# Retention ahead of a gated feed-forward block: the first six chunks in blocks of 64 tokens, values scaled in place of keys, and the first weights loaded on 128 partitions and earlier

## The chip, the cores and the metric

The kernel runs on one core of one Trainium2 chip. The metric is device microseconds of one execution. Before the change three runs gave a median of 663.18 us (662.83 to 664.07). The profile is of one execution of its own.

The engines are named as in the profile: PE is TensorE's matrix products and PEld its weight loads, DVE is VectorE, ACT is ScalarE, POOL is GpSimd, SP is SyncE, which issues most transfers. Each engine works through its own queue in the order in which the program issued it, and waits for others through semaphores.

## What is computed

```python
# retention: batch 4, 8 heads, 768 tokens, head width 64
gamma = 1.0 - 2.0 ** (-5.0 - np.arange(H))
for t in range(S):
    state = gamma[None, :, None, None] * state + np.einsum('bhd,bhe->bhde', k[:, :, t], v[:, :, t])
    y[:, :, t] = scale * np.einsum('bhd,bhde->bhe', q[:, :, t], state)
# the heads side by side give x: 3072 tokens x 512
h = x @ w_in                      # w_in 512 x 2048
sp = np.maximum(h, 0.0) + np.log1p(np.exp(-np.abs(h)))
out = (h * erf(sp)) @ w_out       # w_out 2048 x 512
```

q, k and v are 32-bit. The two weights are 64-bit floats, and the kernel has to turn them into 32-bit ones itself.

## The kernel before

**Retention.** The 24 chunks of 128 tokens are numbered j = 0 to 23, six to a batch (NC = 6); the first four (JPC = 4) make up the first 512 tokens (TCH) of the feed-forward block. A chunk is computed as scores (keys times queries), a mask, a product of masked scores with values, a product of the running state with queries, and an addition of keys times values to the state. The decay of the heads is put in by scaling keys by one factor and queries by another, per token and head (kq_s), so that the mask has only ones and zeros.

Chunks 0 to 3 are done whole: ret_scale (K_) scales keys and queries on DVE, ret_transpose (T) turns each by four PE transposes and one ACT copy, ret_scores (S_) does eight products of 128x128, ret_mask (M) two DVE operations of 128x512, ret_out (O_) the products with state and values, the state additions and two ACT copies into xT (XC), and ret_add (A) adds to the state on DVE. Their order is written out by hand: the scores of a chunk are issued ahead of the results of the chunk before it. keep_warm issues idle products into one bank.

Chunks 4 and 5 are done in halves of 64 tokens (sub_begin, sub_states, sub_results, sub_sums): 64x64 products, four of which use the array at a time, two states to a chunk, and results of which one part is kept aside in a bank and added by DVE (sub_sums). From chunk 6 on, keys and queries come in blocks of 32x32 by 32 small transfers a chunk (load_blocks, from j = NB = 6), DVE scales them (prepared: the keys for the state, the key blocks, the query blocks) and transposes them, and each chunk is one visit (sub_visit), in which TensorE also does the scores of the chunk after it.

**Feed-forward.** The first 512 tokens are done plainly: hidden (hidden_of, block ft of 128 of the 2048 hidden units) in 16 blocks, four to a group g, then project. hidden_of for blocks 0 and 1 takes the first 384 tokens before the fourth chunk is done and the last 128 after it. From group 4 (G0) on, tokens come in 256 at a time with sums of weights and inputs in place of some of the products (hidden_steps, project_part), and each group of these has one visit.

**Weights.** load_piece brings a piece of W_in (two blocks ft) or W_out into one of four raw buffers; conversion turns a piece into 32-bit floats by five DVE operations (lines 313, 317, 322, 325 and 331 of the listing) and one ACT activation, a Relu on line 314, which reads what the first DVE operation wrote and is read by the fourth. Piece 0 is converted in four parts, two halves of its rows for each block. A raw buffer is loaded again (load_pieces_after) when its conversion has read it. These steps are taken one at a time (pace) between other DVE work, and need("in", ft) takes as many as are missing.

**Order of transfers.** SP issues, in order: keys and queries of chunk 0; then for each further chunk its keys and queries and the values of the chunk before; W_in's piece 0, first block, then the values of chunk 3, then piece 0, second block; pieces 1 to 3; chunk 4. W_in goes to 64 partitions at a time, rows 0 to 255 in the lower half and 256 to 511 in the upper, which goes with the order in which heads are put into xT.

The order in the head, as it stands in the code (one row for what follows one another there):

```python
K_(0, 0); second_scales(); T(0, 0); keep_warm(2); K_(0, 1); T(0, 1); keep_warm(1)
K_(1, 0); T(1, 0); S_(0); K_(1, 1); T(1, 1); keep_warm(2); other_scales(); M(0); S_(1)
K_(2, 0); T(2, 0); O_(0); M(1); K_(2, 1); T(2, 1); A(0); K_(3, 0); O_(1, next_scores)
T(3, 0); K_(3, 1); A(1); T(3, 1); O_(2, lambda: next(weight_steps)); S_(3)
need("in", 0); A(2); M(3); need("in", 1)
ret_out(JPC - 1, lambda: hidden_of(0, slice(TCH - C)), state_last=True)
```

Of the kernel before, what the change touches and what calls it, by code (L numbers as in the profile page):

```python
# [136 lines left out]
def kernel(  # L137
# [42 lines left out]

    def load_blocks(to, src):


        for s, d in itertools.product(range(2), range(2)):
            part = slice((2 * s + d) * 32, (2 * s + d + 1) * 32)
            for u in range(HP):
                nc.sync.dma_start(
                    to[part, u * C : (u + 1) * C].rearrange("p (a d) -> p a d", d=32),
                    src[2 * u + s, :, d * 32 : (d + 1) * 32].rearrange("(a p) d -> p a d", p=32),
                )  # L190

    def load(j):
# [15 lines left out]
        for i, src in enumerate((k, q) if j < NB else ()):  # L208
            nc.sync.dma_start(KQ[j][:, i], src[b, :, now, :].rearrange("h p d -> p h d"))
# [46 lines left out]
    def load_piece(n, *parts):  # L256
# [3 lines left out]
        if which == "in":  # L260
            rows = (slice(2), slice(2, 4)) if n == 0 else (slice(4),)
            for part, g, r in itertools.product(parts or (None,), rows, range(2)):
                f = slice(2 * P) if part is None else slice(part * P, (part + 1) * P)
                nc.sync.dma_start(
                    w[r * D : (r + 1) * D].rearrange("p (g f) -> p g f", g=n_k)[:, g, f],
                    w_in[r * DH : (r + 1) * DH, i * 2 * P : (i + 1) * 2 * P].rearrange(
                        "(g p) f -> p g f", p=D
                    )[:, g, f],
                )
# [134 lines left out]

    for j in range(1, JPC):
        load(j)
        load_values(j - 1)
    load_piece(0, 0)
    load_values(JPC - 1)
    load_piece(0, 1)  # L410
    for n in range(1, 4):
# [4 lines left out]
    causal = const.tile([P, C], F32, name="causal")  # L416
    nc.gpsimd.memset(causal, 1.0)
    nc.gpsimd.affine_select(
        out=causal, in_=causal, compare_op=ALU.is_ge, fill=0.0,
        base=0, pattern=[[1, C]], channel_multiplier=-1,  # L420
    )

    causal_d = const.tile([P, D], F32, name="causal_d")
    for r in range(2):
        own = slice(r * D, (r + 1) * D)
        nc.gpsimd.tensor_copy(causal_d[own], causal[own, own])
    state = const.tile([P, HP, D], F32, name="state")


    state_1 = const.tile([P, HP, D], F32, name="state1")  # L430
    state_2 = loads.tile([P, HP * C], F32, name="kb", bufs=2)[:, : HP * D]
    state_2 = state_2.rearrange("p (u d) -> p u d", d=D)
    mid = [state, state_1, state_2, state, None, state_1]
    adds_of = {JPC: range(2), JPC + 1: range(1), JPC + 2: range(1)}
    assert (JPC + 2) % NC == 0 and NC > 1


    unscale = 1.0 / math.sqrt(D)

    def query_scale(c):  # L440
        nc.vector.reciprocal(kq_s[:, c, 1], kq_s[:, c, 0])
# [20 lines left out]
    kq_b = const.tile([P, NC, 2, HP, 4], F32, name="kq_b")  # L462
    by_b = const.tile([P, 2, HP], F32, name="by_b")

    def load_block_scales():
        for s, d in itertools.product(range(2), range(2)):
            part = slice((2 * s + d) * 32, (2 * s + d + 1) * 32)
            for u in range(HP):
                nc.sync.dma_start(
                    kq_b[part, 0, 0, u],  # L470
                    decay_k[:, 2 * u + s : 2 * u + s + 1].rearrange("(a p) h -> p (a h)", p=32),
                )
        nc.sync.dma_start(by_b[:, 1], decay_s)

    def block_scales():
        nc.vector.reciprocal(by_b[:, 0], by_b[:, 1])
        nc.vector.reciprocal(kq_b[:, 0, 1], kq_b[:, 0, 0])
        nc.vector.tensor_scalar(kq_b[:, 0, 1], kq_b[:, 0, 1], unscale, None, op0=ALU.mult)
        for c in range(1, NC):
            nc.gpsimd.tensor_tensor(  # L480
                kq_b[:, c], kq_b[:, c - 1], by_b[:, :, :, None].to_broadcast([P, 2, HP, 4]),
                op=ALU.mult,
# [3 lines left out]
    QT, KT, SC, AM, XC, SU = {}, {}, {}, {}, {}, {}  # L486
# [4 lines left out]
    idle = ps_o.tile([P, P], F32, name="o0")  # L491

    def keep_warm(n):
        for _ in range(n):
            nc.tensor.matmul(idle, ident, ident, start=True, stop=True)

    keep_warm(7)
# [8 lines left out]
    def ret_scale(j, i=None):  # L506
# [3 lines left out]
        scaled.add(j)  # L510
        part = slice(i, i + 1) if i is not None else slice(2)
        x = KQ[j][:, part]
        by = kq_s[:, j % NC, part, :, None].to_broadcast([P, x.shape[1], H, D])
        nc.vector.tensor_tensor(x, x, by, op=ALU.mult)
        pace(-1.1)

    def ret_transpose(j, part=None):
        assert j in scaled
        for i, (name, store) in enumerate((("k", KT), ("q", QT))):
            if part not in (None, i):  # L520
                continue
            p = ret_psum((ps_h if i else ps_r) if early else None)
# [10 lines left out]
    def prepared(j):  # L533

        if j >= NJ:
            return
        nc.vector.tensor_tensor(
            KQ[j][:, 0], KQ[j][:, 0],
            kq_s[:, j % NC, 0, :, None].to_broadcast([P, H, D]), op=ALU.mult,
# [3 lines left out]
        for i, x in enumerate(blocks):  # L543
            x = x.rearrange("p (u a d) -> p u a d", u=HP, d=32)
            by = kq_b[:, j % NC, i, :, :, None].to_broadcast([P, HP, 4, 32])
            nc.vector.tensor_tensor(x, x, by, op=ALU.mult)
            yield
# [5 lines left out]
    def ret_scores(j, pool=None):  # L553
        pp = SC[j] = [ret_psum(pool) for _ in range(2)]
        for hp in range(HP):
            for s in range(2):
                nc.tensor.matmul(  # L557
                    pp[s][:, hp, :],
                    KT[j][s * D : (s + 1) * D, hp, :],
                    QT[j][s * D : (s + 1) * D, hp, :],  # L560
                    start=True,
                    stop=True,
                )
        pace(1)

    def ret_mask(j):
        AM[j] = ret.tile([P, 2, HP, C], F32, name="am")
        for s in range(2):
            nc.vector.tensor_tensor(
                AM[j][:, s], SC[j][s], causal[:, None, :].to_broadcast([P, HP, C]), op=ALU.mult  # L570
            )
        pace(-1.2)

    def ret_out(j, between=None, state_last=False):
        c = j % NC
        m, i = divmod(j, JPC)
        if i == 0:
            XC[m] = ret.tile([P, HP, TCH], F32, name="xT")

        if early:  # L580
            pp = [ps_o.tile([P, HP, C], F32, name=f"o{(2 * j + r + 1) % 4}") for r in range(2)]
        else:
            pp = [ret_psum() for _ in range(2)]

        def place(h):
            return pp[h % 2][h // 4 * D : (h // 4 + 1) * D, h % 4 // 2, :]

        if state_last:
            between()


        if c:
            for u in PAIRS:
                for r in range(2):
                    h = 2 * u + r
                    own = slice(r * D, (r + 1) * D)
                    nc.tensor.matmul(
                        place(h), state[own, u, :], QT[j][own, u, :],
                        start=(h % 4 < 2), stop=False, skip_group_check=True,
                    )  # L600
        if between is not None and not state_last:
            between()
        for h in (0, 4, 1, 5, 2, 6, 3, 7):
            nc.tensor.matmul(  # L604
                place(h), V[j][:, h, :], AM[j][:, h % 2, h // 2, :],
                start=(not c and h % 4 < 2), stop=True, skip_group_check=True,
            )
# [105 lines left out]
    def sub_visit(j, g):  # L713
# [44 lines left out]
        if c:  # L758
            of_state(0)
# [590 lines left out]
```

## Time and profile before

| what | us |
|---|---|
| median of three runs | 663.18 |
| span of the profiled execution | 660.9 |
| PE busy (share of the span) | 655.7 (99%) |
| DVE busy | 508.4 (77%) |
| ACT busy | 280.2 (42%) |
| POOL busy | 11.7 (2%) |

| stretch, us from the start | what runs in it | PE busy | DVE busy | ACT busy | DMA, GB/s |
|---|---|---|---|---|---|
| 0 to 31.7 | chunks 0 to 3, hidden blocks 0 and 1 | 29.37 | 23.02 | 11.86 | 204 |
| 31.7 to 164 | the rest of the first 512 tokens, chunks 4 to 6 | 132.30 | 122.79 | 73.11 | 158 |
| 164 to 627 | groups with a visit | 462.95 | 343.90 | 187.68 | 51 |
| 627 to 660.9 | the last projections | 31.07 | 18.65 | 7.54 | 31 |

A busy PE is one whose products overlap without a gap by the profile; it says where PE doesn't wait, not that it works at its peak. In the rows of the timeline the columns are the start, the length, the engine, the line, the operation, what it writes and reads, the tile, how many were merged into the row, and in brackets how long the engine was idle before it and who ended that. A 32-bit product stands in the trace as two records, a transpose as one. Starts that lie less than a length apart are pipelined: the distance of two starts is what one more of them costs.

### The profile page before, as it was taken

How to read it: one execution, taken by the hardware profiler on the slowest of the kernel's cores; microseconds unless marked ns; L12 is line 12 of the kernel's file. 1: busy time of each engine (PE TensorE's matmuls, PEld its weight loads, DVE VectorE, ACT ScalarE, POOL GpSimd, SP SyncE). 2: the span in 40 equal slices, each digit the busy share in tenths (PEclk: the TensorE clock that was granted, in tenths of full speed). 3: DMA queues.
4: the chain of work that ended last, by engine and by line, in shares of the span. 5: the costliest groups of instructions: out<-in, count | busy, mean ns of one | idle time of the engine just before them, and what ended most of it. 6: DMA issues, size and time to landing. Idle time of an engine off the chain costs nothing.

```text
span 660.9 us, 15247 instructions
## 1 busy us (share of the span) xinstructions
PE 655.7 (99%) x6200; PEld 557.3 (84%) x6200; DVE 508.4 (77%) x1102; ACT 280.2 (42%) x402; POOL 11.7 (2%) x29
## 2 busy tenths in 40 slices
PE   8999999999999999999999999999999999999998
PEld 7744444576999999999999999999999999999997
DVE  5999999969986786788678678677687688476464
ACT  3468363445534334244254253342432542533440
POOL 1000000110100000000000000000000000000000
PEclk9999999999999999999999999999999999999999
DMA  9999844385753321222222322221231210000000
GB/s 188 223 264 231 211 129 107 63 152 90 144 123 61 85 47 32 67 47 46 70 44 47 73 39 46 42 72 37 44 79 36 46 53 1 2 34 0 1 33 32
DMA packets 159413, 51.88 MB, mean 78 GB/s; under 512 B 143216, under 2 KB 149744, under 8 KB 159344
## 3 DMA queue, kind: packets, MB, share of 16 engines
q1 hardware_dynamic: 157776, 46.72, 32.8%
q0 software_dynamic: 1152, 4.19, 3.4%
q8 instruction: 48, 0.79, 0.5%
q14 instruction: 21, 0.17, 0.1%
q10 hardware_dynamic: 416, 0.01, 0.0%
HBM read 40.39 MB, written 6.29 MB: 71 GB/s over the span
## 4 chain that ended last, share of the span: by engine, by line
PE 98%; DMA 1%; DVE 0%; ACT 0%; issue 0%
PE o L1034 37%; PE hp L951 22%; PE r L951 12%; PE hp L860 8%; PE o L896 8%; PE hp L980 2%; PE r L736 2%; PE hp L628 1%; PE o L772 1%; PE r L524 1%; PE r L557 1%; PE o L604 1%; PE r L751 1%; PE hp L751 1%; DMA kq<-in_k_dram 1%; PE r L772 0%
## 5 line engine op out<-in xcount | busy, mean ns | idle before, releaser
L1034 PE MATMUL o<-w_out_sb,h 128*128 128x256 f32 (+1 forms) x640 | 142.7, 380 | 0.0
L951 PE MATMUL hp<-xs,w_in_sb 128*128 128x128 f32 x988 | 138.1, 275 | 0.0
L1034 PEld LDWEIGHTS o<-w_out_sb,h 128*128 128x128 f32 x640 | 119.5, 190 | 16.6
L963 DVE TENSOR_TENSOR h<-h,hp 128x256 f32<-128x256 f32 x190 | 78.0, 418 | 70.5 <-PE hp L951 65.6
L951 PEld LDWEIGHTS hp<-xs,w_in_sb 128*128 128x128 f32 x988 | 128.4, 192 | 3.0
L1034 PE MATMUL o<-w_out_sb,e 128*128 128x256 f32 x480 | 113.5, 379 | 0.0
L1034 PEld LDWEIGHTS o<-w_out_sb,e 128*128 128x128 f32 x480 | 86.8, 190 | 9.4
L817 ACT ACTIVATE e<-h 128x2048 f32<-128x2048 f32 x22 | 42.1, 1912 | 119.6 <-DVE h L963 119.6
L963 DVE TENSOR_TENSOR h<-h,r 128x256 f32<-128x256 f32 x152 | 56.9, 415 | 22.3 <-PE r L951 21.4
L965 ACT COPY h<-hp 128x256 f32<-128x256 f32 x38 | 14.2, 373 | 130.7 <-PE hp L951 122.7
L951 PE MATMUL r<-xs,w_in_sb 128*128 128x128 f32 x456 | 63.3, 275 | 0.0
L951 PEld LDWEIGHTS r<-xs,w_in_sb 128*128 128x128 f32 x456 | 57.0, 192 | 0.0
L860 PE MATMUL hp<-xT,w_in_sb 128*128 128x512 f32 (+2 forms) x144 | 56.5, 548 | 0.0
L849 DVE TENSOR_TENSOR e<-h,e 128x1024 f32<-128x1024 f32 x42 | 49.2, 1213 | 8.0 <-ACT e L830 8.0
L860 PEld LDWEIGHTS hp<-xT,w_in_sb 128*128 128x128 f32 x144 | 25.8, 190 | 27.0 <-issue 24.6
L951 PE MATMUL hp<-xT,w_in_sb 128*128 128x128 f32 x304 | 46.3, 275 | 0.0
L951 PEld LDWEIGHTS hp<-xT,w_in_sb 128*128 128x128 f32 x304 | 41.5, 192 | 1.4 <-issue 0.5
L830 ACT ACTIVATE e<-e 128x2048 f32<-128x2048 f32 (+1 forms) x23 | 42.1, 1836 | 0.2
L967 ACT ACTIVATE h<-hp 128x256 f32<-128x256 f32 x57 | 21.9, 384 | 29.7 <-PE hp L951 28.3
L951 PE MATMUL r<-xT,w_in_sb 128*128 128x128 f32 x228 | 31.7, 275 | 0.0
L830 ACT ACT_TABLE_LOAD x24 | 30.8, 1283 | 0.4
L951 PEld LDWEIGHTS r<-xT,w_in_sb 128*128 128x128 f32 x228 | 28.5, 192 | 0.0
(164 smaller groups left out, 799.0 us busy)
## 6 DMA issues: line engine op xcount, KB each, us to landing
w_out_sb<-in_moe_w_out_dram SPq DMA_DIRECT2D x14, 512.0 KB, 5.2
kq<-in_k_dram SPq DMA_DIRECT2D x23, 256.0 KB, 4.0
v<-in_v_dram SPq DMA_DIRECT2D x23, 256.0 KB, 3.4
out_dram<-r SPq DMA_DIRECT2D x23, 256.0 KB, 2.9
kq<-in_q_dram SPq DMA_DIRECT2D x288, 16.0 KB, 1.9
kb<-in_k_dram SPq DMA_DIRECT2D x288, 16.0 KB, 1.8
w_in_sb<-in_moe_w_in_dram SPq DMA_DIRECT2D x8, 512.0 KB, 10.1
w_out_sb<-w_out_sb POOLq DMA_DIRECT2D x8, 512.0 KB, 5.3
```

The source lines that it names most:

```text
L736: nc.tensor.matmul(pp[r][col * D : (col + 1) * D, u % 2, t], x[own, u, :], QT[j][own, u, t], start=first(r, col), stop=True, skip_group_ch ...
L751: nc.tensor.matmul(other[a][own, u % 2, D:] if crossed else pp[a][own, u % 2, t], V[j][t, 2 * u + r, :], AM[j][t, r, u, :D], start=crossed ...
L817: nc.scalar.activation(E[g], HS[g], AF.Softplus)
L830: nc.scalar.activation(E[g][:, half], E[g][:, half], AF.Erf)
L849: nc.vector.tensor_tensor(E[g][:, half], HS[g][:, half], E[g][:, half], op=ALU.mult)
L860: nc.tensor.matmul(HP_[ft][:, t], w_in_of(ft, kk), XC[0][:, kk, t], start=(kk == 0), stop=(kk == n_k - 1),)
L896: nc.tensor.matmul(O[0][tt].rearrange("p (d c) -> p d c", d=2), E[g][:, u * TCH + tt * P : u * TCH + (tt + 1) * P], w_out_of(ft), start=(f ...
L951: nc.tensor.matmul(to[:, u, :], w_in_sb[:, s, w, u * P : (u + 1) * P], XS[m](x), start=first and u == 0, stop=True, skip_group_check=True,)
L963: nc.vector.tensor_tensor(h, h, of, op=ALU.add if plus else ALU.subtract)
L965: nc.scalar.copy(h, of)
L967: nc.scalar.activation(h, of, AF.Copy, scale=-1.0)
L1034: nc.tensor.matmul(O[m][i][:, half, at], G[g][a][:, u * P : (u + 1) * P], w_out_sb[:, s, OUT[b], u, at], start=i not in started, stop=(s = ...
```

## The change

All chunks are now done in halves of 64 tokens, with the same functions (score_banks, scores, additions, sub_masks, sub_adds, sub_results, sub_sums). Chunks 0 to 3 are issued one after the other. For them the crossed values go first into the bank of the results, ACT reads one element of it, and then states and straight values are added in the same bank, so that no sum is left to DVE; a function given as "between" is issued after that read. keep_warm takes a new tile in the first bank at each call. The values are scaled in place of the keys (V[j] in ret_scale and prepared), so that the keys can be transposed as they come, and the key blocks need no scaling any more; a small transfer of their factor is gone, and POOL makes it by two copies. Four states are kept in turn in place of three.

W_in goes to 128 partitions, one transfer for each part in place of two; to fit this, the heads are taken in another order (head, slot), and keys and queries of chunks 0 to 5 are loaded by two transfers each (load_heads). W_in's piece 0, both blocks, is issued ahead of chunk 3. Values are issued after the keys and queries of their own chunk. In a visit the additions and scores of the next chunk come first, then all results of this one. The result banks of a visit are those that were the banks of the next scores before, and the other way round. sub_sums of chunk 4 comes two steps earlier, together with the states of chunk 5.

```diff
+    def load_heads(to, src):
+        for s in range(2):
+            nc.sync.dma_start(to[:, s * HP : (s + 1) * HP], src[s::2].rearrange("h p d -> p h d"))
...
-            for part, g, r in itertools.product(parts or (None,), rows, range(2)):
+            for part, g in itertools.product(parts or (None,), rows):
                 f = slice(2 * P) if part is None else slice(part * P, (part + 1) * P)
                 nc.sync.dma_start(
-                    w[r * D : (r + 1) * D].rearrange("p (g f) -> p g f", g=n_k)[:, g, f],
...
+                    w.rearrange("p (g f) -> p g f", g=n_k)[:, g, f],
+                    w_in[:, i * 2 * P : (i + 1) * 2 * P].rearrange("(g p) f -> p g f", p=P)[:, g, f],
                 )
...
+    load_values(0)
     for j in range(1, JPC):
+        if j == JPC - 1:
+            load_piece(0, 0, 1)
         load(j)
-        load_values(j - 1)
-    load_piece(0, 0)
-    load_values(JPC - 1)
-    load_piece(0, 1)
+        load_values(j)
...
+        for i in range(2) if i is None else (i,):
+            scaled.add((j, i))
+            x = KQ[j][:, 1] if i else V[j]
+            by = kq_s[:, j % NC, i, :, None].to_broadcast([P, H, D])
+            nc.vector.tensor_tensor(x, x, by, op=ALU.mult)
+            pace(-0.6)
...
+    def sub_begin(j, pool=None):
+        score_banks(j, pool)
+        scores(j)
+        additions(j)
+        pace(1)
...
+        if between is not None:
+            values(True)
+            nc.scalar.copy(idle_out, pp[0][:, 0, D : D + 1])
+            between()
+        if j % NC:
+            of_state(0)
+        values(False)
+        if between is None:
+            values(True, aside=True)
+        of_state(1)
...
+        score_banks(j + 1)
+        additions(j + 1)
+        scores(j + 1)
+        sub_results(j)
+        sub_states(j + 1)
+        sub_sums(j)
...
-                    waiting.append((sub_states, 5))
-                elif g == 2 and tt == 2:
-                    waiting.append((sub_sums, 4))
+                    waiting.extend(((sub_states, 5), (sub_sums, 4)))
```

The order in the head is now:

```python
T(0, 0); K_(0, 1); keep_warm(2); T(0, 1); K_(0, 0); keep_warm(1)
sub_begin(0); second_scales(); sub_masks(0); T(1, 0); sub_adds(0); K_(1, 1)
sub_results(0, lambda: keep_warm(1)); T(1, 1); K_(1, 0); other_scales()
sub_begin(1); sub_masks(1); sub_adds(1, slice(1)); K_(2, 1)
sub_results(1, lambda: T(2, 0)); sub_adds(1, slice(1, 2)); K_(2, 0); T(2, 1)
sub_begin(2); sub_masks(2); sub_adds(2, slice(1)); next(weight_steps)
sub_results(2, lambda: keep_warm(1)); T(3, 0); need("in", 0)
sub_adds(2, slice(1, 2)); K_(3, 1); hidden_of(0, first); T(3, 1); K_(3, 0)
need("in", 1); hidden_of(1, first, slice(2)); sub_begin(3, ps_r); sub_masks(3)
hidden_of(1, first, slice(2, 3)); sub_adds(3)
sub_results(3, lambda: hidden_of(1, first, slice(3, 4)))
```

K_(j, 0) scales the values of chunk j, K_(j, 1) its queries, T(j, 0) transposes its keys and T(j, 1) its queries; first is the first 384 tokens.

## The prediction

> **What bounds the kernel now.** I read the chain of waits first, then TensorE's waits before and after 60 us, then busy time by stretch, then the first 37 us engine by engine.
>
> ```profile
> span 660.9 us, 15247 instructions
> PE 98%; DMA 1%; DVE 0%; ACT 0%; issue 0%
> ```
>
> The chain is TensorE almost alone. So the time is the start of its unbroken run plus the work in that run. Its waits, first those within 60 us:
>
> ```profile
> PE o L495 <- POOL ident masks.py:199: 1.5, 1, 1.5
> PE o L597 <- DVE state L806: 0.3, 1, 0.3
> PE r L524 <- DVE kq L514: 0.3, 1, 0.3
> PE r L557 <- ACT qT L530: 0.2, 1, 0.2
> ```
>
> The same view from 60 us to the end is empty. A change can thus move the time in two ways: by TensorE work after the head, or by the moment at which the head is done. As the mark of that moment I take the first 512-wide product of weight block 2:
>
> ```profile
> 27.27 7.25 PE L860 MATMUL hp<-xT,w_in_sb 128*128 128x384 f32 x30
> 31.74 1.50 PE L860 MATMUL hp<-xT,w_in_sb 128*128 128x512 f32 x3
> ```
>
> From 31.74 us TensorE does not pause again. The columns of the next view are the stretch, then busy us of PE, PEld, DVE, ACT and POOL, the clock, the DMA share, GB/s:
>
> ```profile
> 25.00:30.00 5.00, 5.00 (x58) 3.52 (x58) 4.83 (x14) 2.38 (x5) 0.00 (x0) 1.00 1.13 231
> 30.00:35.00 5.00, 5.00 (x25) 3.31 (x24) 4.86 (x11) 2.36 (x4) 0.00 (x0) 1.00 1.14 234
> 40.00:45.00 5.00, 5.00 (x13) 2.22 (x12) 4.72 (x9) 4.89 (x5) 0.00 (x0) 1.00 1.00 354
> ```
>
> VectorE is as full as TensorE here: it converts the 64-bit weights, five operations a block. Its queue:
>
> ```profile
> 19.37 0.29 DVE L313 TENSOR_SCALAR w_out_sb<-w_out_sb 128x256 uint32<-128x256 uint32 x1 [0.35 <-DMA w_out_sb<-in_moe_w_in_dram]
> 22.52 0.43 DVE L325 SCALAR_TENSOR_TENSOR w_out_sb<-w_out_sb 128x256 uint32<-128x256 uint32 x1 [0.35 <-ACT w_out_sb L314]
> 30.30 0.69 DVE L331 SCALAR_TENSOR_TENSOR w_in_sb<-w_out_sb,xs 128x512 f32<-128x512 f32 x1
> 33.35 0.69 DVE L331 SCALAR_TENSOR_TENSOR w_in_sb<-w_out_sb,xs 128x512 f32<-128x512 f32 x1
> ```
>
> Conversion starts at 19.37, when its weights land, and then idles 0.35 us in all. Block 2 is ready at 30.99 (30.30 + 0.69), 0.75 us ahead of its use at 31.74. So the head has two limits within a microsecond of each other, and 0.75 us is all that a later VectorE may cost for nothing.
>
> **The change, part by part.** *TensorE work in chunks 0 to 3.* A chunk of 128 took 1.09 (scores, 15.49 to 16.58), 0.92 (values), 0.57 (state additions) and 0.60 (state products): 3.18 us, 2.58 without state products. In blocks of 64, by the rows of chunks 4 and 5, it is 0.51 scores, 0.58 additions, 0.46 values, 0.52 state products: 2.07, and 1.81 for chunk 0. That is 0.77 + 3 x 1.11 = 4.1 us less, and one idle product (0.2 to 0.4) less. It counts only where TensorE waits for nothing else.
>
> *VectorE work in the head.* Eight scalings of 0.6 remain (values instead of keys). Eight masks go from 0.6 apart to 0.33; state additions go from four to eight of about 0.35; the reciprocals of the other chunks go from one of 0.35 to four of 0.20. Sum: -2.2 + 1.4 + 0.45, about nothing. What matters is where it stands in the queue.
>
> *Order.* Before, the scores of a chunk were issued ahead of the results of the one before. Now each chunk runs alone: transposes, ScalarE copy, scores and additions, masks, values, results. I walk the four queues with the durations above and 0.03 to 0.16 us from an end to who waits. Scores start at 8.0, 12.8 and 17.8; a round of chunk 1 is scores and additions 12.8 to 13.9, masks from 14.0, values from 14.8, keys of chunk 2 transposed to 15.7, states and values to 16.45, queries transposed to 17.0, ScalarE's two result copies and then the query copy to 17.8. A round is 5.0 us with 1.8 us of TensorE waiting. Masks of chunk 2 end at 19.8 and the first conversion starts at 20.1. The earlier load of W_in (it would land near 17) buys nothing, since conversion stands behind those masks: 0.7 us later than 19.37.
>
> *What stands between conversion and block 2.* Before, from 19.37 to 30.99, the queue also held one state addition (0.33) and two masks (1.2): 1.5 us, with 0.5 idle (0.35 in the row at 22.52, the rest at 20.42). Now it holds three additions (1.1), two scalings of chunk 3 (1.2) and two masks (0.7): 3.0, so 1.5 more. And it waits four times. Conversion's second operation on ScalarE (L314 before) now stands in ScalarE's queue behind a transpose copy that is behind two result copies: 1.0 us at 22.7. Again behind the query copy of chunk 3, which TensorE can transpose only after the first hidden block: 0.7 at 27.0. The masks of chunk 3 wait for scores that TensorE issues only after half of hidden block 1, itself waiting for weights: 0.9 at 30.2. And behind the result copies of chunk 3: 1.2 at 34.1. Together 3.8, against 0.5. Block 2 is ready at 30.99 + 0.7 + 1.5 + 3.3 = 36.5; the walk itself, step by step, gives 36.7. TensorE, which has by then done both first hidden blocks and their last 128 columns (to 36.4), starts at 36.7 where it started at 31.74: 5.0 us later. Its 4.1 us saved are lost in these waits.
>
> *Loads.* The key and query loads of six chunks become 24 issues on SP for 12 (0.44 each at the start), W_in's 28 become 14 (0.6 each), and one small scale load goes; four of W_in's are moved past chunk 3's three loads. POOL gets two small copies and five products of half the size, first wanted at 122: nothing. The page's loads were in flight 4 to 5 us and came 1.2 us apart, so issue hides behind the queue; chunk 0's second halves land as before (4.34 for keys). If that cover were gone, 0.45 us twice. W_in on 64 partitions ran at 231 to 234 GB/s, W_out at 354 in the window from 40. For 128 partitions I bound it by these two; either lands block 1's weights before 27 us, and they are wanted at 32.6: nothing on the path. Chunk 3's loads slip behind W_in's 1 MB by 3 to 4.5 us, to some 20 to 23, and are wanted at 21.9 (keys) and 24.8: 0 taken, 1 at worst.
>
> *New small waits.* The one-element ScalarE read after the crossed values: 0.2, as the 128x1 copy at 3.05; covered by the idle product or transposes, except in chunk 2 (0.6, in the walk). A fresh bank for idle products makes them wait for TensorE itself: no row, 0 to 0.2 three times, I take 0.1.
>
> *After the head.* A visit has the same 112 or 128 small products in another order; no wait is there to lose and the operands are ready a group earlier: 0, bounded by 0.2 either way for each of 17 if one order packs worse (the visit at 304.88 takes 1.79 for 112). Eighteen key-block scalings (0.6 each) leave VectorE: nothing, it is busy 344 of 463 us there. Values, loaded last, are now scaled first: the wait at 139.30 was for that load's neighbour, so 0 to 0.3. The W_out block needed at 84.6 was ready at 83.7 (its last step, 82.46 + 1.23); VectorE slips 0.6 more than TensorE, so 0.3 remain: 0 taken, 0.4 at worst.
>
> Sum: 31.74 to 36.7, plus 0.1 to 0.3 of small waits: +5.2. The profiled execution would go from 660.9 to 666.1; the median of the runs is 2.3 above that span, and 663.18 + 5.2 = 668.4.
>
> *The clock.* The first 14 idle records take 3.36 us, 0.24 each; the same product from 9.89 on takes 0.11, and in between, four records from 6.02 take 0.85 and four from 6.87 take 0.52. [...] By the rows TensorE stays busy from 1.5 to 7.5 us as before (slow records fill it), and I keep 7 us. [...]
>
> **The rivals.** *TensorE alone sets the head (faster).* If ScalarE let the conversions through and masks came at once, the head would cost its TensorE work: 36.7 less the 9.0 us of waits in my walk is 27.7, so 31.74 - 27.7 = 4.0 us sooner, 659.2. For it: TensorE's queue hardly waits today. Against it: VectorE has 23 us of work of its own between 2.9 and 36.7, most of it in an order in which it can't start early. It decides if block 2 is converted by 28 us.
> *A draw.* If only the four waits vanish, VectorE is 0.7 + 1.5 - 0.5 late, less 0.75 of cover: about +1; with the rounds shortened by 1 as well it is nothing, 663.2.
> *Slower still: late loads.* Eleven loads 1.2 apart from 4.34 are in at 16.4, and 256 KB of W_in at 234 GB/s take 1.1, yet conversion waited until 19.37: W_in's first packets cost 1.9 us more than their bytes. If chunk 2's values or chunk 3's keys are caught in that, each microsecond past 16 or 22 goes straight into conversion: +2, 670.4.
> *The visits cost.* 17 x 0.2 = 3.4 more: 671.8; the packing of like rows speaks against it.
>
> **How the numbers follow.** Forecast (conversion late) 0.66; late loads or clock 0.15; visits 0.04; draw 0.05; faster 0.10. The forecast's own range is 666.5 to 669.8 (the waits behind ScalarE vary by their order, 0.5 each). Reaching to late loads and part of the draw: 665.2 to 671.0. A measurement of this kernel can tell 0.2% (1.3 us) from no change: faster 0.10, same 0.05, slower 0.85.
>
> **What would show it.** First conversion near 20.1 us; VectorE waiting three times for ScalarE's relu of conversion (L325 of the new file) by 36 us; first 512-wide product near 36.7; no TensorE wait after it; group length 25.9 as before; W_in faster than 300 GB/s without use. I am wrong if that product starts before 33, or if visits change the length of a group.

## The result, and the profile after

The changed kernel takes 670.09 us (median of 4 runs, 669.69 to 671.59), the kernel before 663.03 in the same session (4 runs, 662.83 to 664.07): ratio 1.011, 95% interval 1.0095 to 1.0124, that is 7.06 us slower. The forecast was 668.4 with a range of 665.2 to 671.0.

The page of the profiled execution, its first line, its row of granted clock in 40 slices, and its chain of waits:

```profile
span 668.5 us, 15750 instructions
...
PEclk9899999999999999999999999999999999999999
...
PE 96%; DVE 1%; ACT 1%; DMA 1%; issue 0%; SPq 0%; DVEq 0%
```

The chain is still TensorE, but one slice (16.7 to 33.4 us) has lost clock, which no slice had before. TensorE's waits up to 60 us, the longest first (sum, times, longest):

```profile
PE hp L754 <- DVE w_in_sb L342: 3.0, 3, 2.1
PE o L640 <- DVE am L596: 2.0, 3, 0.9
PE r L569 <- ACT qT L544: 1.8, 3, 0.7
...
PE hp L754 <- ACT xT L676: 0.5, 1, 0.5
```

Before, these waits came to 0.8 us but for the 1.5 us for the identity at the start. Now TensorE waits for converted weights, for masks and for ScalarE's copies. The same view from 60 us on is empty, as before. TensorE's rows around the mark that the prediction used:

```profile
28.84 2.68 PE L754 MATMUL hp<-xT,w_in_sb 128*128 128x384 f32 x4 [2.09 <-DVE w_in_sb L342]
31.45 1.14 PE L569 MATMUL r<-qT,kT 64*64 64x64 f32 x32
32.36 0.70 PE L579 MATMUL r<-e 64*64 64x64 f32 x32
...
39.00 6.25 PE L754 MATMUL hp<-xT,w_in_sb 128*128 128x512 f32 x14 [0.34 <-DVE w_in_sb L342]
```

The first 512-wide product of block 2 starts at 39.00 in place of 31.74. Taking the start of the same product in both traces, the offset is 7.26 there, 7.29 from 54 to 136 us, 7.31 up to 170, 7.44 after the first visit, 7.59 to 7.62 from 216 (the kernel before's time) to 583, and 7.43 at the end. So the head makes the difference, and the seventeen visits together less than 0.2.

VectorE's rows in the head, with what ended its idle time in brackets:

```profile
20.31 0.28 DVE L324 TENSOR_SCALAR w_out_sb<-w_out_sb 128x256 uint32<-128x256 uint32 x1
23.81 0.42 DVE L336 SCALAR_TENSOR_TENSOR w_out_sb<-w_out_sb 128x256 uint32<-128x256 uint32 x1 [0.89 <-ACT w_out_sb L325]
27.81 0.43 DVE L336 SCALAR_TENSOR_TENSOR w_out_sb<-w_out_sb 128x256 uint32<-128x256 uint32 x1 [0.71 <-ACT w_out_sb L325]
33.12 0.75 DVE L596 TENSOR_TENSOR am<-r,causal 128x256 f32<-128x256 f32 x2 [2.76 <-PE r L579]
37.44 0.69 DVE L336 SCALAR_TENSOR_TENSOR xs<-w_out_sb,xs 128x512 uint32<-128x512 uint32 x1 [1.38 <-ACT xs L325]
```

These are the first conversion and the four waits of the forecast: 1.0, 0.7, 0.9 and 1.2 were predicted, 0.89, 0.71, 2.76 and 1.38 are there. The one that is off is the masks of chunk 3. ScalarE's rows ahead of the second and the last of these waits show the relu of conversion (L325) directly behind copies that had waited for TensorE:

```profile
26.78 0.58 ACT L544 COPY qT<-r 128x512 f32<-128x512 f32 x1 [3.00 <-PE r L538]
27.26 0.51 ACT L325 ACTIVATE w_out_sb<-w_out_sb,below 128x256 uint32<-128x256 uint32 x1
...
36.14 0.65 ACT L676 COPY xT<-o 128x256 f32<-128x256 f32 x2 [1.47 <-PE o L653]
36.67 0.73 ACT L325 ACTIVATE xs<-xs,below 128x512 uint32<-128x512 uint32 x1
```

Busy time by stretch, with the clock behind POOL's column, shows what happened in front of them:

```profile
28.50:29.00 0.50, 0.16 (x1) 0.19 (x2) 0.50 (x3) 0.07 (x1) 0.00 (x0) 1.00 1.09 348
29.00:30.00 1.00, 1.00 (x2) 0.44 (x2) 0.93 (x4) 0.44 (x1) 0.00 (x0) 0.53 1.11 345
...
32.00:32.50 0.50, 0.50 (x32) 0.50 (x28) 0.00 (x0) 0.00 (x0) 0.00 (x0) 0.52 1.29 226
32.50:33.00 0.50, 0.50 (x37) 0.43 (x29) 0.00 (x0) 0.00 (x0) 0.00 (x0) 1.00 1.30 224
```

The clock was granted at half from 29.07 to 32.48, just after the wait of 2.09 us. Four records of 128x384 take 2.68 there and 1.56 a few us earlier.

### The profile page after: what moved, and what is told of

Same layout as the page of the kernel before. It is cut to its first block, busy times and chain, and to the rows that moved or that the text cites. A ratio compares the mean times of both kernels' runs of the same rounds, so it can differ in the third digit from the quotient of the medians.

```text
span 668.5 us, 15750 instructions
## 1 busy us (share of the span) xinstructions
PE 655.4 (98%) x6454; PEld 554.7 (83%) x6454; DVE 496.8 (74%) x1092; ACT 280.3 (42%) x406; POOL 10.9 (2%) x30
## 4 chain that ended last, share of the span: by engine, by line
PE 96%; DVE 1%; ACT 1%; DMA 1%; issue 0%; SPq 0%; DVEq 0%
PE o L924 37%; PE hp L841 22%; PE r L841 11%; PE o L786 8%; PE hp L754 8%; PE hp L870 2%; PE r L579 2%; PE r L569 2%; PE hp L640 1%; PE hp L653 1%; DMA kq<-in_q_dram 1%; PE r L538 0%; ACT xT L676 0%; PE o L640 0%; PE o L653 0%; ACT qT L544 0%
## 5 line engine op out<-in xcount | busy, mean ns | idle before, releaser
L754 PE MATMUL hp<-xT,w_in_sb 128*128 128x512 f32 (+2 forms) x144 | 59.0, 560 | 3.5 <-DVE w_in_sb L342 3.0
L596 DVE TENSOR_TENSOR am<-r,causal 128x256 f32<-128x256 f32 x43 | 16.4, 419 | 20.1 <-PE r L569 12.5
```

Source lines behind the costliest of these rows:

```text
L596: nc.vector.tensor_tensor(AM[j][:, s], SC[j][s][:, :, :D], causal[:, None, :].to_broadcast([P, HP, D]), op=ALU.mult,)
L754: nc.tensor.matmul(HP_[ft][:, t], w_in_of(ft, kk), XC[0][:, kk, t], start=(kk == 0), stop=(kk == n_k - 1),)
```

## The experiments

Every kernel ran beside the kernel before on the same chip; the sessions were on different chips, so the ratios compare better than the medians. "Offset" is how much later TensorE starts the first output products (54.4 us in the kernel before) in the profiled execution of each, which need not be the median run.

| run | median, us | ratio to before (95%) | offset, us |
|---|---|---|---|
| changed kernel | 670.09 | 1.0110 (1.0095 to 1.0124) | 7.29 |
| w_in_last | 671.39 | 1.0130 (1.0113 to 1.0146) | 7.73 |
| idle_fill | 669.25 | 1.0094 (1.0079 to 1.0109) | 5.68 |
| conv_early | 669.07 | 1.0090 (1.0075 to 1.0105) | 6.52 |
| copy_early | 668.30 | 1.0082 (1.0067 to 1.0097) | 5.90 |
| both_early | 666.21 | 1.0053 (1.0041 to 1.0065) | 3.30 |
| best (new order) | 667.72 | 1.0066 (1.0043 to 1.0088) | 5.16 |
| best_v | 667.93 | 1.0072 (1.0046 to 1.0097) | 6.47 |
| best_w | 669.10 | 1.0094 (1.0081 to 1.0107) | 5.57 |
| more_products | 669.41 | 1.0107 (1.0085 to 1.0129) | 6.12 |
| wide_head | 664.57 | 1.0026 (1.0014 to 1.0037) | 1.00 |
| wide_v_last | 664.00 | 1.0014 (1.0005 to 1.0024) | 1.15 |
| changed_again | 670.69 | 1.0113 (1.0095 to 1.0131) | 7.84 |

### w_in_last: the moved load undone

```diff
-        if j == JPC - 1:
-            load_piece(0, 0, 1)
         load(j)
         load_values(j)
+    load_piece(0, 0, 1)
```

> One move of the change undone: both blocks of W_in's piece 0 are issued behind chunk 3's three loads again, all else as in the changed kernel (670.1 us, first conversion at 20.31 us, first 512-wide product at 39.00). Theory (conversion is held by the order of VectorE's queue: it stands behind the masks of chunk 2, which end at 20.3): the first conversion stays at 20.3 within 0.3, the first 512-wide product at 39.0 within 0.7, and the time at 670.1 within 0.7. Rival (loads: the queries of chunk 3 landed at 21.9 and the values at 22.8, behind 1 MB of W_in, and set the end of the head): the loads of chunk 3 land some 3 us sooner and the time falls by about 2, to 668. Rival (the early W_in is of use): W_in lands 3 to 4 us later, conversion starts near 21 to 22, and the time rises by 1 to 2.

671.39 us, and first conversion at 20.75. It stood behind the masks of chunk 2 again, which were 0.45 later themselves (19.75 for 19.30), and it waited for no transfer; the four relu and mask waits are the same (0.89, 0.71, 2.77, 1.39). So what the two load rivals rest on didn't happen. The time itself missed the theory's 670.1 within 0.7 and lies where the second rival had it: 1.3 above the changed kernel's median, with overlapping intervals. In the profile 0.44 of it is that late start and 0.6 a later wait (wide_v_last, below).

### idle_fill: the clock

```diff
     T(3, 1)
     K_(3, 0)
+    keep_warm(8)
```

> Eight idle products (16 records of 0.11 us, 1.8 us at full clock) are put into the 2.09 us for which TensorE waited at 28.84 in the changed kernel; nothing else. Theory (the clock, granted at half from 29.07 to 32.48 in the profile, made the masks of chunk 3 wait 2.76 us where 0.9 was forecast): the clock stays whole, the four records of hidden block 1 take 1.56 again (2.68 in the changed kernel) and the scores 0.53 (0.90), the masks wait about 1.3, the first 512-wide product comes at 37.5 and the time falls by up to 1.5, to 668.6 to 669.3. Rival (the drop is an accident of the profiled run: two other runs with clock 1.000 gave 669.7 and 669.95): the time stays within 0.4 of 669.8, with the clock at 1.000 in all runs.

669.25 us, clock 1.000 in all four runs. TensorE's rows of this run:

```profile
26.64 1.95 PE L509 MATMUL o<-ident 128*128 128x128 f32 x16
28.80 1.56 PE L754 MATMUL hp<-xT,w_in_sb 128*128 128x384 f32 x4 [0.21 <-DVE w_in_sb L342]
30.29 0.69 PE L569 MATMUL r<-qT,kT 64*64 64x64 f32 x32
...
37.39 2.81 PE L754 MATMUL hp<-xT,w_in_sb 128*128 128x512 f32 x6 [0.34 <-DVE w_in_sb L342]
```

Useless work made the head 1.61 us shorter: the same products start at 28.80 and 28.84, and the masks wait 1.09 in place of 2.76. So in the profiled execution the half clock was the size that the forecast lacked. In the median the gain is 0.84, with intervals that overlap. The changed kernel's clock doesn't drop in every run (changed_again, below), and its two runs at a mean clock of 1.000 still take 669.69 and 669.95, within 0.7 of idle_fill's median. So the drop doesn't account for the median, and the rival's point stands in part: what made those two runs as long was not traced.

### conv_early, copy_early, both_early: two waits that cover each other

```diff
     T(2, 1)
+    for _ in range(4):
+        next(weight_steps)
     sub_begin(2)
     sub_masks(2)
     sub_adds(2, slice(1))
-    next(weight_steps)
```

That is conv_early; copy_early is

```diff
     T(3, 0)
-    need("in", 0)
     sub_adds(2, slice(1, 2))
     K_(3, 1)
-    hidden_of(0, first)
     T(3, 1)
+    need("in", 0)
+    hidden_of(0, first)
```

and both_early has both.

> The first four steps of the conversion of W_in are issued ahead of the scores and masks of chunk 2, into the 2.65 us for which VectorE waited there (16.7 to 19.3); nothing else. Both accounts expect the first conversion at 16.7 in place of 20.31. Theory (ScalarE's queue: the relu of the second half of block 0 would still stand behind the copy of chunk 3's queries, which TensorE can transpose only after the first hidden block): the wait in front of that step grows from 0.71 to about 2.7, the first 512-wide product comes only about 0.85 sooner and the time is 669.2 within 0.6. Rival (the amount of work in VectorE's queue sets the head): 1.7 to 3.5 us sooner, 666.6 to 668.4.

> The transposes of chunk 3's queries, and with them ScalarE's copy of them, are issued ahead of the last conversion steps of block 0 and ahead of hidden block 0, where they were behind it; the second state addition and the query scaling of chunk 3 go with them; conversion starts where it did. Theory (ScalarE's queue): the relu no longer waits behind that copy, the waits of VectorE for ScalarE's relu before block 2 fall from 2.98 in all to about 1.6, the first 512-wide product comes about 1.4 us sooner and the time is 668.7 within 0.6. Rival (the loads: the queries of chunk 3 landed at 21.9): VectorE waits for them instead, and the time stays at 670.1 or rises.

> The first four conversion steps ahead of the scores of chunk 2, and the transposes and copy of chunk 3's queries ahead of hidden block 0, together. Each alone gave little (669.1 and 668.3 us, for 670.1 in the changed kernel): started early, VectorE waited 4.07 us for the relu behind the query copy; with the copy early, conversion still began at 20.5. Theory (the two waits cover each other: the head needs the early start and the free ScalarE queue): together they give more than their sum of 2.8, the first 512-wide product comes near 34.5 to 35.8 (39.00 in the changed kernel) and the time is 666.0 within 0.8. Rival (additive, each shortens its own wait): 667.3. Rival (chunk 3's loads, behind W_in, are the bound then: its queries landed at 21.9): no better than the better of the two, 668.3.

VectorE's longest wait for the relu in conv_early (row of the timeline, the wait in brackets):

```profile
28.64 0.43 DVE L336 SCALAR_TENSOR_TENSOR w_out_sb<-w_out_sb 128x256 uint32<-128x256 uint32 x1 [4.07 <-ACT w_out_sb L325]
```

And in copy_early:

```profile
25.76 0.42 DVE L336 SCALAR_TENSOR_TENSOR w_out_sb<-w_out_sb 128x256 uint32<-128x256 uint32 x1 [1.80 <-ACT w_out_sb L325]
```

Conversion that begins 3.4 us sooner (16.93) gains 0.77 in the first 512-wide product and 1.0 in the median: 4.07 us are lost behind the copy of chunk 3's queries. 2.7 was forecast for that wait, right in kind and short in size. copy_early gained 1.8 in the median, more than the 1.4 forecast, but not by the waits that were to fall: the relu behind the query copy is gone, the first one waits 1.80 for 0.89, and they sum to 3.19. In its profile the gain is at the masks of chunk 3 (1.15 for 2.76), since the half clock came earlier (20.92 to 24.34). Both together gained 3.9, against 2.8 for the sum of the two: 666.21 where 666.0 was forecast. By the ratios it is 3.8 against 3.2, a difference inside the intervals, and in four of its five runs the mean clock is 0.999 or more. So a gain beyond the sum isn't shown by the times. That one wait hid the other is shown by the rows: the 4.07 us that conv_early lost behind the query copy are not there in both_early. VectorE then waits 0.85 for chunk 3's queries, so the loads begin to show. A new line stands among TensorE's waits of both_early:

```profile
PE o L640 <- issue: 0.7, 1, 0.7
```

"Issue" is a wait for nothing that the profile shows.

### best, best_v, best_w: the head in a new order

From the scores of chunk 2 on, the new order reads:

```python
sub_begin(2); K_(3, 1); sub_masks(2); T(3, 0); sub_adds(2); K_(3, 0)
sub_results(2, lambda: (T(3, 1), next(weight_steps), next(weight_steps)))
sub_begin(3, ps_r)
for _ in range(2): next(weight_steps)
sub_masks(3); sub_adds(3); hidden_of(0, first, slice(2))
sub_results(3, lambda: (next(weight_steps),))
need("in", 0); hidden_of(0, first, slice(2, 4)); hidden_of(0, slice(TCH - C, TCH))
need("in", 1); hidden_of(1, slice(TCH))
```

Before that, T(j + 1, 0) stands behind the masks of chunk j and T(j + 1, 1) is what its results take as "between". W_in is loaded as in w_in_last.

> All parts of the change kept (blocks of 64, values scaled, W_in on 128 partitions, the visits), only the order of the head written anew: keys and queries of the next chunk are transposed while the masks of this one are made, its query scaling stands ahead of the state additions, the relu of conversion ahead of the result copies; chunk 3 is finished ahead of the conversion of block 1; W_in is loaded behind chunk 3; hidden blocks 0 and 1 are taken 512 wide. Walked through the queues with the durations of the rows: rounds of 3.6 to 4.3 us in place of 5.0, masks of chunk 2 end at 18.0 (20.06 in the changed kernel), conversion runs from 19.4 almost without a wait, block 2 is ready at 30.5, where it was 30.99 before the change and 38.85 after it. Theory (the order makes the 7 us, not the parts): 662.6 within 0.8, about the kernel before. Rival (the parts: smaller blocks put more single operations into VectorE's queue, whatever the order): not below 666. Rival (the 4.1 us of TensorE work saved come through in full): 659.2.

> As the run with the new order of the head, and from chunk 6 on the values are loaded ahead of the keys and queries of their chunk. In the changed kernel VectorE waited 3.88 and 3.96 us for values that are issued last of 34 transfers and scaled first; TensorE lost 0.17 us by it there, and 0.4 to 1.0 in the variants in which the head was shorter. Theory: both waits vanish, TensorE's offset to the kernel before is constant from the first 512-wide products to the end but for 0.13 at the first visit, and the time is 0.3 to 0.9 below the run without this. Rival (the wait only moves to the key or query blocks, which now land later): no difference beyond 0.2.

> As the run with the new head order and values loaded first, but W_in's piece 0 (1 MB) ahead of chunk 3's loads, as the change had it. In the changed kernel this made no difference that showed (W_in behind chunk 3 gave 671.4 for 670.1, the other way if anything). Theory (what a load's place is worth depends on what waits for it: with the shorter rounds chunk 3's queries are wanted at 16.4 and land near 21): conversion starts some 3 us later by the queue, block 2 too, and the time is 3 us above the run before it, 665 to 666. Rival (loads are hidden in either place): the same time within 0.5. Rival (early W_in helps now): below it.

667.72 us, five above the theory, with runs from 663.94 to 669.72. TensorE's two longest waits in the profile of best:

```profile
PE r L578 <- issue: 2.6, 1, 2.6
PE o L639 <- DVE state L609: 2.0, 1, 2.0
```

And the rows of TensorE's timeline at the first of them:

```profile
22.28 0.63 PE L578 MATMUL r<-e 64*64 64x64 f32 x27
25.51 0.33 PE L578 MATMUL r<-e 64*64 64x64 f32 x5 [2.60 <-issue]
```

TensorE stops after 27 of 32 like products, with no wait that the profile shows. The first stop ends at 20.04, 0.96 after the VectorE operation to which the view puts it down (18.64 to 19.08). Counting TensorE's records (products, weight loads and semaphore waits, from 0), the stops stand before records 705 and 961, 256 apart, in best and in best_v, and before 705 in both_early. One queue on the page of best fits that number (packets, MB, share of the DMA engines):

```profile
q8 instruction: 50, 0.82, 0.5%
```

50 packets, 0.82 MB: 16 KB each, which divided by 256 records is 64 bytes for each. In best such packets moved from 16.50 to 18.92 and from 23.19 to 24.15, and TensorE went on at 20.04 and 25.51, 1.1 and 1.4 us after each. The number of such packets goes with TensorE's records: 48 for 12,487 in the kernel before, 50 for 12,979 in the changed kernel, 48.8 and 50.7 times 256. That they carry TensorE's instructions is inferred from this and from the queue's name. The packet of the second stop began to move at 23.19, after TensorE had stopped at 22.91; why so late isn't shown. After the second stop came half clock, from 26.68 on (clock 0.78 from 25 to 28 us, 0.65 from 28 to 31).

best_v told nothing in its time, since the stops (2.1 and 3.4 us there) hide what it tries; its trace shows the rival right. The waits for values are gone, VectorE waits 10.2 us for key blocks in their place, and TensorE's offset grows by 0.33 between 142 and 165 us. best_w came 1.2 above best_v where 3 was forecast, with overlapping intervals: VectorE waits 5.9 us for chunk 3's queries and TensorE 3.2 for its keys, in place of the stops rather than on top of them. So the early W_in does bring waits once the order is tight enough; that it costs time isn't shown.

### more_products and wide_head: instructions

```diff
     T(1, 0)
+    more = [ps_o.tile([P, P], F32, name=f"o{s}") for s in range(2)]
+    for i, a, s in itertools.product(range(8), range(2), range(2)):
+        own = slice(s * D, (s + 1) * D)
+        nc.tensor.matmul(more[s][a * D : (a + 1) * D, :D], ident[own, :D], ident[own, :D], start=True, stop=True)
```

> The run with the new order of the head (667.7 us, stops of TensorE at 18.06 before its 706th record, the first product of chunk 2's results, and at 22.91 before its 961st, within chunk 3's additions), plus 32 idle products of 64x64 (128 records, about 1 us) after the transposes of chunk 1's keys, into a time in which TensorE waits for masks. Theory (instructions come in blocks of 256 and TensorE stops where a block ends): the stops stay at the 706th and 961st record, which are now 128 records earlier in the program: within the scores of chunk 2 and within the results of chunk 2. Rival (the stops belong to what is computed there: masks, the values of chunk 3, a bank): they stay before chunk 2's results and within chunk 3's additions, at records 834 and 1089. Time by the theory 667 to 670 (a stop is as long as the fetch is late, and the block is used up 0.5 to 1.5 us sooner); by the rival 667.7 to 668.7.

TensorE's waits of more_products that are put down to nothing:

```profile
PE o L652 <- issue: 3.4, 2, 2.1
...
PE r L568 <- issue: 1.4, 2, 1.0
```

Four stops in more_products now, before records 449, 705, 961 and 1217: 256 apart each time, and within the scores of chunks 1 and 2 and the results of chunks 2 and 3. The two stops of best moved 128 records up the program, as the theory said; what is computed there has no part in it.

In wide_head the four chunks have the kernel before's scores, masks and results of 128 tokens, in its order. W_in's piece 0 is loaded around chunk 3's values as before, and from chunk 6 on the values come first in the loads, as in best_v. All else is as changed; for example:

```diff
-                t, own = slice(a * D, (a + 1) * D), slice(s * D, (s + 1) * D)
-                nc.tensor.matmul(
-                    SC[j][s][t, hp, :D], KT[j][own, hp, t], QT[j][own, hp, t], start=True, stop=True,
+            own = slice(s * D, (s + 1) * D)
+            nc.tensor.matmul(
+                SC[j][s][:, hp, :], KT[j][own, hp, :], QT[j][own, hp, :], start=True, stop=True
```

> Chunks 0 to 3 in blocks of 128 tokens again, in the order of the kernel before (scores of a chunk ahead of the results of the one before); every other part of the change stays (values scaled, W_in on 128 partitions, heads' order, visits), the values come first in the loads from chunk 6 on, and W_in's piece 0 stands around chunk 3's values as before. The head has 144 TensorE records a chunk for 272. Theory (in the run with the new order TensorE stopped for 2.0 and 2.6 us at its 706th and 961st record for want of instructions: fetches of 16 KB, 256 instructions of 64 bytes, began at 16.5 and 23.2 and TensorE went on 1.1 to 1.4 us after they had landed; blocks of 64 need twice the instructions): no such stop, the first hidden blocks follow as before the change, and the time is 663.5 within 0.7. Rival (the other parts of the change cost something in the head): 665 or more. Rival (blocks of 64 are not the cost, the order was): as the run with the new order, 667 to 668.

664.57, with no line for "issue" and the clock whole in all six runs. Its offset is 1.00 us at the first output products, 2.02 from 164 us on. So 1.0 is the price of what is left of the change in this head; no run splits it further. Most of the other 1.0 is the wait that loading the values first had brought (best_v): VectorE waits 7.4 us for key blocks up to 145.29, and TensorE 0.7 for VectorE. It missed the forecast of 663.5 within 0.7 by 0.4.

### wide_v_last: the values' place

```diff
-        nc.vector.tensor_tensor(
-            V[j], V[j], kq_s[:, j % NC, 0, :, None].to_broadcast([P, H, D]), op=ALU.mult
-        )
-        yield
         blocks = (KB[j], KQ[j][:, 1].rearrange("p h d -> p (h d)"))
...
             nc.vector.transpose(store[j].rearrange("p u t -> p (u t)"), x)
             yield
+        nc.vector.tensor_tensor(
+            V[j], V[j], kq_s[:, j % NC, 0, :, None].to_broadcast([P, H, D]), op=ALU.mult
+        )
+        yield
```

> As the run with chunks 0 to 3 in blocks of 128 (664.6 us; offset of its TensorE work to the kernel before 1.00 us at the first output products, 2.02 from 164 us on, where VectorE had waited for key blocks that land later when the values are loaded first), but the loads from chunk 6 on in the order of the change, and of the four steps that prepare a chunk the scaling of the values comes last in place of first. Theory (a step that needs the transfer issued last must not be the first in VectorE's queue): no wait for a transfer reaches TensorE, the offset stays at 1.0 plus the 0.15 of the first visit to the end, and the time is 663.7 within 0.5. Rival (the transposes, which need the key blocks issued just before the values, then wait instead): the offset grows by 0.3 to 1.0 between 142 and 216 us as in the other runs, and the time is 664.2 to 664.9.

From wide_head it also differs in the loads from chunk 6 on, which are in the order of the change again. 664.00 us. The offset is 1.15 from 54 to 136 us, 1.38 to 1.40 from the first visit to 583 and 1.22 at the end, without the growth by 1.0 that wide_head has. The wait aimed at is this one of the changed kernel's VectorE:

```profile
146.83 0.69 DVE L551 TENSOR_TENSOR v<-v,kq_s 128x512 f32<-128x512 f32 x1 [3.88 <-DMA v<-in_v_dram]
216.19 0.69 DVE L551 TENSOR_TENSOR v<-v,kq_s 128x512 f32<-128x512 f32 x1 [3.96 <-DMA v<-in_v_dram]
```

The load of these values is the last of 34 issues (212.01) and lands at 216.17. TensorE lost 0.17 by it there, 0.39 in idle_fill, 0.64 in conv_early, 0.97 in copy_early, and nothing in both_early and best. In wide_v_last VectorE still waits 2.4 and 2.0 us for loads, now at the transposes, as the rival had it, but TensorE loses nothing by it at the second.

### changed_again

The kernel is the changed one as it is.

> The changed kernel once more, to see why its runs at a mean clock of 1.000 (spans 668.0 and 668.2) were hardly shorter than its profiled run with the clock at half from 29.07 to 32.48 (668.5), though the idle products that kept the clock whole moved the first 512-wide product from 39.00 to 37.39. Theory (the time at which the clock is first granted in full differs from run to run, 5.2 to 7.4 us in the profiles here, and the runs without the later drop are those with the late first grant): runs with a mean clock of 0.997 have spans of 668.3 to 669.9, runs with 1.000 of 667.0 to 668.3, and the median of all is 670.1 within 0.7. Rival (the drop costs nothing in the time and the idle products gained by something else): no difference between runs with and without it.

670.69 us. Over both sessions, spans at a mean clock of 1.000 are 667.4, 668.0 and 668.2; at 0.997 they are 668.5, 668.9 and 669.1; at 0.994, 669.7 and 669.9. So the runs with a drop are about 1 us longer for each 0.003 of mean clock, and the rival falls; by estimate 0.003 is one stretch at half clock as long as the 3.41 us of the first profile (0.5 x 3.41 of 668.5). But the spans at 1.000 are still 6.5 to 7.3 above the 660.9 of the kernel before, so most of the difference is there without any drop. That the runs without it have the late first grant isn't shown: both profiles of this kernel, at a mean clock of 0.997, have the drop. Among TensorE's waits of the second profile is one that the first had not:

```profile
PE o L640 <- issue: 0.7, 1, 0.7
```

It stands before record 705. So the changed kernel as it is has one of these stops in one of its two profiles.

## Why the prediction was right, point by point

The path is the one forecast: conversion starts late, waits in VectorE's queue, and with it block 2. The size is short. The measured 670.09 lies above the forecast's own range (666.5 to 669.8) and inside the wide one, whose upper part had been kept for late loads or a late clock. Neither came in that form; the half clock that did come was not foreseen. That the time still fell inside the wide range is partly luck.

- *The mark and what sets it.* Right: VectorE's block 2 sets TensorE's start (0.34 us waited at 39.00), and after it the offset to the kernel before moves by less than 0.4 us in 630.
- *Order and rounds.* Right: scores of chunks 1 and 2 at 12.82 and 18.01 (12.8, 17.8), first conversion at 20.31 (20.1).
- *The earlier W_in buys nothing.* Right for this order: w_in_last has no wait for it. In the tight order of best_w it brings waits.
- *VectorE's four waits.* The relu behind ScalarE's copies: 0.89, 0.71 and 1.38 for 1.0, 0.7 and 1.2. That the copies made the second is shown by conv_early (4.07) and copy_early (gone); for the other two only the order in ScalarE's rows shows it (for the first, copies from 22.21 and the relu at 23.27). **The mis-sized term is the masks of chunk 3**, 0.9 forecast and 2.76 measured in the profiled execution. The half clock makes 1.5 of the 1.9: 1.12 in the records of hidden block 1 (2.68 for 1.56) and the rest in the scores. idle_fill, without it, has 1.09. With 0.2 from the late start and 0.2 from the last wait this is the way from 36.7 to 39.00, and from +5.2 to +7.1 there. For the two runs at a mean clock of 1.000, which are as much as 6.7 and 6.9 above the kernel before, the cause of what goes beyond 5.2 stays open; in idle_fill's profile, with the whole clock, the offset is 5.68 in the head and 6.02 at the end.
- *The clock.* The forecast asked only when full clock is first granted and kept 7 us: 5.17 in this kernel's profile, which is no later. What a later full grant would cost, for which a part of the chance of 0.15 was kept, no run shows. It didn't ask whether half clock could come again after a wait of 2 us; by changed_again such a stretch goes with about 1 us.
- *After the head.* Visits: 0.13 at the first, 0.00 at those after it, 0.16 back at the end, well inside 17 x 0.2. Values scaled first: 0 to 0.3 was given, 0.17 measured in this kernel, up to 0.97 in others; the mechanism was named, but the size depends on the moment.
- *Loads.* Right for the changed kernel: W_in on 128 partitions came 512 KB each 1.5 to 1.6 us (25.26, 26.78, 28.27, 29.84), 330 to 350 GB/s, and nothing waited for it.
- *The rival "TensorE alone" (659.2).* Its condition, conversions let through and masks at once, was tried in best. What stood in the way there was first of all not VectorE's 23 us but the stops of 2.0 and 2.6 us and the half clock after them: 274 records a chunk in blocks of 64, and 256 records in 5.47 us from going on at the first stop to going on at the second (20.04 to 25.51). A round of the changed kernel, 5.2 us from the scores of chunk 1 to those of chunk 2, is already there. No order tried here had the 4.1 us of TensorE work saved; that none can isn't shown (one run of best took 663.94).

No version here beats the kernel before. The nearest, wide_v_last, is 1.0 us slower (1.0005 to 1.0024). Two parts of the change that the title names are not in it: the blocks of 64 in the first four chunks, with their order, and W_in ahead of chunk 3; and it scales the values last.

## What to carry to other kernels

When work is cut into smaller products, count instructions as well as time: TensorE's stops lay 256 records apart here, at 274 records a chunk; wide_head, with 144, has no line for "issue". A stall had a second price in two profiles: 3.41 us at half clock came after the wait of 2.09 us in the changed kernel, and half clock after the stop of 2.60 us in best. In idle_fill's profile, idle products in the wait were cheaper than the wait alone. Two waits in series on one queue can hide each other: conversion 3.4 us sooner gained 0.77 us while the second wait stood.

## What the runs showed of the hardware

- **Stops 256 records apart.** Stops of TensorE before records 449, 705, 961 and 1217 in more_products, before 705 and 961 in best and best_v, before 705 in both_early and changed_again. In best they ended 1.1 and 1.4 us after a 16 KB packet of the queue that the page calls "instruction" had landed, and from going on at the first (20.04) to going on at the second (25.51) it took 5.47 us, at a DMA share of 0.99 from 20 to 25 us. The profile calls such a stop "issue", or puts it down to the last semaphore (the first one of best).
- **Half clock.** In the changed kernel's profile half clock lasted 3.41 us (29.07 to 32.48). Taken in stretches of that length from the first full grant at 5.17, TensorE was busy for 0.62, 0.90, 0.55, 0.80, 0.68, 0.84 and 0.39 of the seven ahead of it; full clock followed the first six, half clock the last (25.65 to 29.07, around a wait of 2.09 us). The 3.41 us ahead of the half clock were busy for 0.34 in best (23.27 to 26.68) and for about 0.54 in copy_early (17.51 to 20.92). From what share on full clock follows isn't shown: after 0.55 it was full in one profile, after about 0.54 half in another. In idle_fill, with idle products in the wait, the clock was 1.00 from 28 to 34 us.
